# Another order of the passes, one streamed weight unit fewer and a ring of five places in a recurrent attention kernel

## The chip, the cores and the metric

The kernel runs on one core of one Trainium2 chip. A core has a matrix engine (TensorE, "PE" in the profile; "PEld" is its weight load), a vector engine (VectorE, DVE), a scalar engine (ScalarE, ACT), GpSimd (POOL) and SyncE (SP), which mostly issues transfers; 16 DMA engines move data between the chip's memory and the core's on-chip memory. Matmuls write to PSUM, eight banks of accumulator memory, from which VectorE and ScalarE copy. The metric is the device time of one execution in microseconds (us); lower is better.

## What is computed

The output is the sum of three things on a sequence of 2048 tokens of 1024 features: the input itself, a memory-augmented recurrent attention, and a dense layer with GELU. Cut to what matters:

```python
def _A_ref(x, mem0, Wq, Wk, Wv, Wo, seg_len):     # seg_len = 32, 64 segments, 32 heads of 128
    mem = mem0                                      # 8 rows
    for s in range(n_seg):
        h = jnp.concatenate([mem, xs], axis=1)      # 8 memory rows + 32 tokens
        q, k, v = (jnp.einsum('btd,dhe->bhte', h, W) for W in (Wq, Wk, Wv))
        scores = jnp.where(mask, jnp.einsum('bhqe,bhke->bhqk', q, k) * scale, -1e9)
        o = jnp.einsum('bhqk,bhke->bhqe', softmax(scores), v)
        o = jnp.einsum('bhte,hed->btd', o, Wo)
        mem = o[:, :M, :]                           # the next segment needs these 8 rows
        outs.append(o[:, M:, :])
xn = layernorm(x)
return x + _A_ref(xn, ...) + (gelu(xn @ w1 + b1) @ w2 + b2)
```

Every segment needs all of Wq, Wk, Wv and Wo (each 1024 x 4096 in bf16, 8 MB), and the memory rows of the segment before. So the 64 segments run one after the other, and 32 MB of weights pass TensorE in each.

## The kernel before, in words

**Stages.** First the layer norm and the dense layer over all tokens (L257 to L515), then the recurrence (L522 on), one segment after the other. The profile sees the recurrence begin some 360 us into the span, when its first weights are fetched.

**Rows.** A segment's "main" rows are 24 of its tokens and the 8 memory rows, 32 in all. Its last 8 tokens, the "left" rows, are done for four segments at once, in a batch of 32 rows: the left keys in a group's segment 0 (i4 = 0), the left queries of the first half of the heads in segment 1, of the second half in segment 2, the left values in segment 3, and the output rows of a batch in segment 1 (`left_o`). A pass with left rows has twice the matmuls.

**Weight units.** The weights are cut into 64 units of 128 x 2048 bf16 (512 KB): eight for each of Q, K and V and each half u of the heads, and 16 for Wo. `ORDER` (L53 to L68) is the order in which a segment uses them: K, Q, V of half 0, then K, Q, V of half 1, then O. Most of them stay on chip. The 18 marked S in `PLACED` (L69) are streamed anew in every segment into a ring of six places (`STREAM_BUFS`, L50): when TensorE is done with a streamed unit, `unit_done` (L575) calls `start_stream` (L207), which issues the transfer of the unit that uses the same place next, on SP's queue (L215). One streamed unit, `IN_PSUM` (L74), lies transposed back in two PSUM banks (`kept`) and is copied to its place by ScalarE and VectorE (L212, L213) in place of a transfer.

**A pass.** `half_pass` (L634) multiplies the rows by eight units, four matmuls of 32 columns of the array side by side for each (L616), into a PSUM bank taken from a list of four (`new_acc`, `let_go`). `at` holds what is issued to the engines behind unit number i of a pass. Rows of K and Q leave PSUM by a ScalarE copy (L664; left rows by VectorE, L670) into a home on chip, where VectorE turns them (L679). The homes are `d_oL` and `b_oL`, which later hold the attention output, and `natQ`.

**Attention of a half.** `scores(u)` (L714) are matmuls into the bank `mixed` (L722, L728), the exponential on ScalarE (L733) and the masks on VectorE (L738); q's left columns come by L702, and L707 (`keep_q`) puts some aside. `sums` (L741) sums over keys by matmuls (L747), inverts by a logarithm and an exponential on ScalarE (L751, L752) and multiplies (L753, L754). `values(u, r)` (L756) multiplies by V, a quarter of the heads at a time, into two fresh banks, whose main and left columns are copied out by two instructions each (L776, L777).

**The order around the change.** scores(0) is issued behind unit 5 of V0, sums behind unit 2 of K1, the values of half 0 behind units 4 and 6 of Q1; scores(1) behind unit 5 of V1, sums of half 1 behind unit 1 of O, its values behind units 4 and 6 of O. Between segments the product's memory rows are copied (L873, L875), transposed by matmuls (`put_mem`, L247) and written into the next segment's rows `hr` (L251); three and three "lead" products of the next left pass (`lead_products`) are issued around them. `hr` has one buffer; its tokens are loaded by a transfer from POOL's queue (L223) issued behind V1.

Of the kernel before, what the change touches and what calls it, by code (L numbers as in the profile page):

```python
# [68 lines left out]
PLACED = "S....S.." "..S...S." "..S...S." "..S....S" "..S..S.." ".S...S.." "S...S..S" "...S..SS"  # L69
# [9 lines left out]
def kernel(  # L79
# [51 lines left out]
    natQ = nc.alloc_sbuf_tensor_at("natQ", [P, 512], BF16, offset=SCRATCH + 2048)  # L131
# [29 lines left out]
    for half in range(2):  # L161
        m = mask_left[0:SEG, :, 8 * half:8 * half + 8]
# [44 lines left out]
    def start_stream():  # L207
        nonlocal started
        if started < len(streams):
            t = slab(STREAM_PLACES[started % STREAM_BUFS])  # L210
            if streams[started] == IN_PSUM and "kept" in nxt:
                nc.scalar.copy(out=t[:, 0:1024], in_=nxt["kept"][:, 0, :])  # L212
                nc.vector.tensor_copy(out=t[:, 1024:2048], in_=nxt["kept"][:, 1, :])  # L213
            else:
                nc.sync.dma_start(out=t[:, :], in_=copies[streams[started]])  # L215
# [19 lines left out]
    b_oL = sp.tile([P, 1152], BF16, name="b_oL")  # L235
    HOME = {"d": d_oL[:, 0:512], "b": b_oL[:, 0:640]}
    o_main = [t.rearrange("p (h t) -> p h t", h=16) for t in (d_oL[:, 0:512], b_oL[:, 128:640])]
    o_both = [t.rearrange("p (t h) -> p h t", h=16) for t in (d_oL[:, :], b_oL[:, 128:1152])]

    def put_mem(o_sb, hT, ps, nb=4):  # L240

        nc_ = KT // nb
        rows = ident[:, :].rearrange("p (j t) -> p j t", j=nb)[:, :, NX:SEG]
        psM = ps[:, 0:8 * KT].rearrange("p (c j t) -> p c j t", c=nc_, j=nb)
        for c in range(nc_):
            for q in range(4):
                nc.tensor.matmul(  # L247
                    psM[32 * q:32 * q + 32, c, :, :], lhsT=o_sb[:, c * P + 32 * q:c * P + 32 * q + 32], rhs=rows,
# [9 lines left out]
    with tc.tile_pool(name="ma", bufs=2) as ma, tc.tile_pool(name="mps", bufs=6, space=PSUM) as mps:  # L258
# [11 lines left out]
        o_sb = HOME["d"]  # L270
        nc.vector.memset(o_sb[:, 0:256], 0.0)
# [10 lines left out]
        for j in range(4):  # L282
            nc.sync.dma_start(out=o_sb[32 * j + NX:32 * j + 32, 0:256], in_=mem0[:, 256 * j:256 * j + 256])
# [67 lines left out]

        def with_left(seg):
# [3 lines left out]
        def turn_R(ttg, small=None):  # L356
# [3 lines left out]
            for i in range(4):  # L360
# [8 lines left out]
                if with_left(seg):  # L369
                    pairs = [(both[w][0:SEG, :, :], halves[w]) for w in range(2)]  # L370
                else:
                    pairs = [(hr_d[seg + 1, :, 256:512].rearrange("(j t) c -> t j c", j=4), rows)]
                for sl in (slot, slot ^ 2) if seg in (0, 1, NSEG - 2, NSEG - 1) else (slot,):
                    r0 = SEG + NL * sl
# [147 lines left out]
    with tc.tile_pool(name="late", bufs=1) as late, \  # L522
# [28 lines left out]
        def keep_unit(t):  # L551

            for n in range(4):
                for k in range(4):
                    nc.tensor.transpose(tr[:, k, :], t[:, 512 * n + P * k:512 * n + P * (k + 1)], ident[:, :])
                turned = HOME["b"][:, 0:512].rearrange("p (k t) -> p k t", k=4)
# [34 lines left out]
        for t in o_both:  # L591
            nc.vector.memset(t[:, :, 32:64], 0.0)
        for s in range(NSEG):
# [13 lines left out]
            og, slot = divmod(s + 2, GRP)  # L607
            st = {}
# [48 lines left out]
            def home(tag, pool=sp):  # L657
                if tag in HOME:
                    return HOME[tag][:, 0:512]
                return natQ[:, :] if tag == "n" else pool.tile([P, 512], BF16, name="natL", tag=tag)[:, :]  # L660

            def rows_out(ps, tag):
                nat = home(tag)
                nc.scalar.copy(out=nat[:, :], in_=ps[:, :])  # L664
                let_go(ps)
                return nat

            def left_out(psL, tag, pool=sp):
                nat = home(tag, pool)
                nc.vector.tensor_copy(out=nat[:, :], in_=psL[:, :])  # L670
                let_go(psL)
                return nat

            def left_values(u, ps):
                VL[u] = left_out(ps, f"VL{u}", late)

            def turn(out, nat):

                nc.vector.transpose(out=out, in_=nat.rearrange("p (h e) -> p h e", e=32))  # L679

            def turn_k(ps):
                st["kT"] = sp.tile([P, 16, 32], BF16, name="kT", tag="a")
                turn(st["kT"][:, :, :], rows_out(ps, "d"))

            def turn_kL(ps, u):
                kL[u] = sp.tile([P, 16, 32], BF16, name=f"kL{u}")
                turn(kL[u][:, :, :], left_out(ps, "d"))

            def turn_q(ps, tag):
                st["qT"] = HOME["b"].rearrange("p (h q) -> p h q", q=40)  # L690
                turn(st["qT"][:, :, 0:32], rows_out(ps, tag))

            def turn_qL(ps, u, tag):
                turn(qL[:, u, :, :], left_out(ps, tag))

            def q_left(u):
# [5 lines left out]
                nc.vector.tensor_copy(out=st["qT"][:, :, 32:40], in_=q)  # L702
# [11 lines left out]
            def scores(u):  # L714

                kT, qT = st["kT"], st["qT"]
                sA = mixed[:, 0:160].rearrange("p (c q) -> p c q", q=40)
                sB = mixed[:, 160:224].rearrange("p (c q) -> p c q", q=16)
                for c in range(4):
                    for j in range(4):  # L720
                        q = slice(32 * j, 32 * j + 32)
                        nc.tensor.matmul(  # L722
                            sA[q, c, :], lhsT=kT[:, 4 * c + j, :], rhs=qT[:, 4 * c + j, :],
                            start=(c == 0), stop=True, skip_group_check=True, tile_position=(0, 32 * j),
                        )
                    for j in range(4):
                        q = slice(32 * j, 32 * j + 32)
                        nc.tensor.matmul(  # L728
                            sB[q, c, :], lhsT=kL[u][:, 4 * c + j, :], rhs=qT[:, 4 * c + j, NX:40],
                            start=False, stop=True, skip_group_check=True, tile_position=(0, 32 * j),  # L730
                        )
                pr = sp.tile([P, 224], BF16, name="pr", tag="e")
# [3 lines left out]
                for p, m in ((prA[:, :, 0:NX], mask_order), (prB, mask_left[:, i4, :])):  # L736
                    n = m.shape[-1]
                    nc.vector.tensor_tensor(out=p, in0=p, in1=m[:, None, :].to_broadcast([P, 4, n]), op=ALU.min)  # L738
                st["prA"], st["prB"] = prA, prB

            def sums():  # L741
                prA, prB = st["prA"], st["prB"]
                dA = mixed[:, 0:160].rearrange("p (c q) -> p c q", q=40)
                for p, d, b in ((prA, dA, True), (prB, dA[:, :, NX:40], False)):
                    for j in range(4):
                        q = slice(32 * j, 32 * j + 32)
                        nc.tensor.matmul(  # L747
                            d[q, :, :], lhsT=bd[:, q], rhs=p, start=b, stop=not b, skip_group_check=True,
                            tile_position=(0, 32 * j),
                        )  # L750
# [3 lines left out]
                nc.vector.tensor_tensor(out=prB, in0=prB, in1=dA[:, :, NX:40], op=ALU.mult)  # L754

            def values(u, r):  # L756

                V, prA, prB = st["V"], st["prA"], st["prB"]
                av = [new_acc() for _ in range(2)]
                oV = [t[:, 0:160].rearrange("p (c q) -> p c q", q=40) for t in av]  # L760
                for c in range(4):
# [6 lines left out]
                    for b in range(2):  # L768
                        q = slice(64 * r + 32 * b, 64 * r + 32 * b + 32)
                        nc.tensor.matmul(  # L770
                            oV[b][:, c, NX:40], lhsT=VL[u][q, c * P:(c + 1) * P], rhs=prB[q, c, :],
                            start=False, stop=True, skip_group_check=True, tile_position=(64 * r + 32 * b, 0),
                        )
                for b, cp in enumerate((nc.scalar.copy, nc.vector.tensor_copy)):
                    hs, t0 = slice(8 * r + 4 * b, 8 * r + 4 * b + 4), SEG + NL * slot
                    cp(out=(o_both if left_o else o_main)[u][:, hs, 0:32], in_=oV[b][:, :, 0:32])  # L776
                    cp(out=o_both[u][:, hs, t0:t0 + NL], in_=oV[b][:, :, 32:40])  # L777
                    let_go(av[b])

            def o_product(unit, t, acc):  # L780
# [3 lines left out]
                lhs = o_both[i // 4] if left_o else o_main[i // 4]  # L784
# [14 lines left out]
            turn_k(psK)  # L799
# [3 lines left out]
            turn_q(psQ, "d")  # L803
            if left_q[0] and first:
                turn_qL(psQL, 0, "d")
            q_left(0)
            psV, psVL = half_pass("V", 0, left_v, {5: [lambda: scores(0)]})
            st["V"] = left_out(psV, "b")
            if first:
                left_values(0, psVL)  # L810


            at = {2: [sums]}
            if left_q[0] and not first:
                at[5] = [lambda: keep_q(0), lambda: turn_qL(psQL, 0, "d")]
            psK1, psK1L = half_pass("K", 1, left_k, at)
            turn_k(psK1)
            if left_k:
                if more and not first:
                    load_left_rows(g + 1, nc.gpsimd)  # L820
                turn_kL(psK1L, 1)
            at = {4: [lambda: values(0, 0)], 6: [lambda: values(0, 1)]}
            if left_v and not first:
                at[6].append(lambda: left_values(0, psVL))
            psQ1, psQ1L = half_pass("Q", 1, left_q[1], at)
            turn_q(psQ1, "n")
            if first:
                turn_qL(psQ1L, 1, "n")
            q_left(1)
            at = {5: [lambda: scores(1)]}  # L830
            if left_q[1] and not first:
                at[2] = [lambda: keep_q(1), lambda: turn_qL(psQ1L, 1, "n")]
# [16 lines left out]
            st["V"] = left_out(psV1, "a")  # L849
# [8 lines left out]
            at = {1: [sums], 4: [lambda: values(1, 0)], 6: [lambda: values(1, 1)]}  # L858
# [12 lines left out]
            if not final:  # L871
                o_sb = HOME["d"]
                nc.scalar.copy(out=o_sb[:, 0:256], in_=psX[:, 0:256])  # L873
                if left_o:
                    nc.vector.tensor_copy(out=o_sb[:, 256:512], in_=psX[:, 256:512])  # L875
# [8 lines left out]
                put_mem(o_sb, nxt["hT"], mixed[:, 256:512], 4 // nw)  # L884
# [81 lines left out]
```

## Time and profile before

| what | value |
|---|---|
| three runs | 2080.75, 2083.34, 2098.01 us; median 2083.34 |
| the profiled execution | 2073.2 us |
| its span, first to last instruction | 2071.5 us |
| mean granted clock of TensorE | 0.98 |
| PE busy | 1814.4 us (88%), 34291 matmuls |
| DVE, ACT, POOL busy | 976.9 (47%), 655.8 (32%), 270.9 us (13%) |
| moved by DMA | 661 MB, mean 319 GB/s |
| chain that ended last | PE 60%, DMA 19%, DVE 9%, ACT 7%, issue 4% |

The profile is of one execution, so durations in it are added up against its own time, not against the median. A row of instructions gives line, engine, operation, output <- input, count, then busy us and mean ns of one, then the idle time of the engine before them and what ended most of it. Since matmuls overlap in TensorE, a mean of 386 ns for a matmul is its passage, not its share of the time. A row of waits gives who waited for whom, in total us, times and the longest one. In the windows, the clock is that granted to TensorE as a share of full speed, and the DMA share is the mean busy share of the 16 DMA engines.

### The profile page before, as it was taken

How to read it: one execution, taken by the hardware profiler on the slowest of the kernel's cores; microseconds unless marked ns; L12 is line 12 of the kernel's file. 1: busy time of each engine (PE TensorE's matmuls, PEld its weight loads, DVE VectorE, ACT ScalarE, POOL GpSimd, SP SyncE). 2: the span in 40 equal slices, each digit the busy share in tenths (PEclk: the TensorE clock that was granted, in tenths of full speed). 3: DMA queues.
4: the chain of work that ended last, by engine and by line, in shares of the span. 5: the costliest groups of instructions: out<-in, count | busy, mean ns of one | idle time of the engine just before them, and what ended most of it. 6: DMA issues, size and time to landing. Idle time of an engine off the chain costs nothing.

```text
span 2071.5 us, 77587 instructions
## 1 busy us (share of the span) xinstructions
PE 1814.4 (88%) x34291; PEld 1034.7 (50%) x34291; DVE 976.9 (47%) x2553; ACT 655.8 (32%) x1540; POOL 270.9 (13%) x528
## 2 busy tenths in 40 slices
PE   6999999978888888888889888879888888888887
PEld 3444444445555555554555555545555555455554
DVE  6665657134444444444444444444444444444443
ACT  4342525113232323232323332223332323232332
POOL 0000000004411111111111111111111111111111
PEclk9999999999999999999999999999999999999999
DMA  9721212899999999999999999999999999999998
GB/s 328 246 56 38 59 39 60 311 343 369 386 369 367 377 360 370 363 388 341 370 363 382 381 369 355 350 366 366 364 370 339 356 352 379 350 367 355 373 361 330
DMA packets 228974, 661.17 MB, mean 319 GB/s; under 512 B 47851, under 2 KB 65211, under 8 KB 228636
## 3 DMA queue, kind: packets, MB, share of 16 engines
q1 hardware_dynamic: 207100, 636.04, 82.4%
q0 software_dynamic: 16000, 16.87, 2.5%
q8 instruction: 268, 4.39, 0.8%
q10 hardware_dynamic: 5536, 3.30, 0.5%
q14 instruction: 70, 0.57, 0.1%
HBM read 641.85 MB, written 31.52 MB: 325 GB/s over the span
## 4 chain that ended last, share of the span: by engine, by line
PE 60%; DMA 19%; DVE 9%; ACT 7%; issue 4%; ACTq 0%; POOL 0%; DVEq 0%; POOLq 0%; SPq 0%
PE acc L616 23%; PE acc L788 12%; PE ps L419 9%; DMA u<-Wc_O 8%; PE ps L467 7%; DMA u<-Wc_Q 4%; ACT d_oL L664 2%; DVE b_oL L679 2%; PE acc L764 2%; DMA res<-hr_d 2%; DMA outM_d<-res 2%; PE ps L500 2%; ACT d_oL L776 2%; DVE d_oL L670 1%; DVE kT L679 1%
## 5 line engine op out<-in xcount | busy, mean ns | idle before, releaser
L616 PE MATMUL acc<-u,hr 128*32 128x512 bf16 x11520 | 808.0, 386 | 41.4 <-DMA u<-Wc_Q 13.8
L616 PEld LDWEIGHTS <-hr 128*32 128x32 bf16 x12288 | 360.2, 97 | 317.8 <-issue 83.7
L616 PE MATMUL acc<-u,hrL 128*32 128x512 bf16 x2880 | 260.5, 388 | 5.0 <-issue 5.0
L664 ACT CAST d_oL<-acc 128x512 bf16<-128x512 f32 x192 | 112.4, 585 | 385.9 <-PE acc L616 316.6
L419 PE MATMUL ps<-u 128*128 128x512 bf16 x896 | 195.4, 381 | 2.6 <-ACT u L325 2.6
L679 DVE STREAM_TRANSPOSE kT<-d_oL 128x512 bf16<-128x512 bf16 x128 | 91.3, 713 | 198.5 <-ACT d_oL L664 198.5
L788 PEld LDWEIGHTS <-b_oL 128*32 128x32 bf16 (+1 forms) x3552 | 141.6, 119 | 60.2 <-issue 49.9
L788 PE MATMUL acc<-u,d_oL 128*32 128x256 bf16 (+1 forms) x2220 | 142.9, 299 | 19.5 <-issue 10.3
L788 PEld LDWEIGHTS <-d_oL 128*32 128x32 bf16 (+1 forms) x3552 | 118.7, 112 | 60.2 <-issue 25.0
L467 PE MATMUL ps<-u 128*128 128x512 bf16 x672 | 147.0, 379 | 0.0
L788 PE MATMUL acc<-W_O,b_oL 128*32 128x256 bf16 (+1 forms) x2220 | 124.1, 308 | 22.7 <-issue 22.7
L419 PEld LDWEIGHTS <-u 128*128 128x128 bf16 x896 | 87.9, 98 | 108.8 <-issue 4.3
L738 DVE TENSOR_TENSOR pr<-pr,beside 128x96 bf16<-128x96 bf16 (+1 forms) x256 | 49.0, 232 | 156.1 <-ACT pr L733 156.1
L733 ACT ACTIVATE pr<-mixed 128x224 bf16<-128x224 f32 x128 | 45.7, 357 | 236.7 <-PE mixed L728 174.8
L616 PEld LDWEIGHTS <-hrL 128*32 128x32 bf16 x3072 | 89.8, 97 | 51.9 <-issue 13.6
L213 DVE COPY u<-kept 128x1024 bf16<-128x1024 bf16 x63 | 43.6, 692 | 146.0 <-ACT u L212 143.5
L467 PEld LDWEIGHTS <-u 128*128 128x128 bf16 x672 | 65.3, 98 | 77.3 <-DVE g_u L435 0.4
L788 PE MATMUL acc<-u,b_oL 128*32 128x256 bf16 (+1 forms) x1332 | 88.2, 309 | 16.4 <-DMA u<-Wc_O 10.2
L223 POOL DMA_DIRECT2D hr<-hr_d x63 | 34.6, 549 | 516.8 <-PE acc L616 325.9
L928 POOL DMA_DIRECT2D out_dram<-res x124 | 63.2, 516 | 254.2 <-DVE res L890 253.3
L427 ACT ACTIVATE g_xb<-ps,b1col 128x512 bf16<-128x512 f32 x112 | 76.8, 686 | 60.4 <-PE ps L419 59.3
L212 ACT COPY u<-kept 128x1024 bf16<-128x1024 bf16 x63 | 63.8, 1012 | 91.3 <-PE acc L788 86.7
(123 smaller groups left out, 2377.5 us busy)
## 6 DMA issues: line engine op xcount, KB each, us to landing
u<-Wc_O SPq DMA_DIRECT2D x384, 512.0 KB
u<-Wc_K SPq DMA_DIRECT2D x256, 512.0 KB
u<-Wc_V SPq DMA_DIRECT2D x256, 512.0 KB
u<-Wc_Q SPq DMA_DIRECT2D x193, 512.0 KB
u<-in_B_w_dram SPq DMA_DIRECT2D x16, 448.0 KB
u<-in_B_w_dram SPq DMA_DIRECT2D x14, 512.0 KB
u<-in_A_Wq_dram SPq DMA_DIRECT2D x12, 512.0 KB
u<-in_A_Wv_dram SPq DMA_DIRECT2D x12, 512.0 KB
```

The source lines that it names most:

```text
L212: nc.scalar.copy(out=t[:, 0:1024], in_=nxt["kept"][:, 0, :])
L213: nc.vector.tensor_copy(out=t[:, 1024:2048], in_=nxt["kept"][:, 1, :])
L419: nc.tensor.matmul(ps[:, :].rearrange("p (s t) -> p s t", t=SEG), lhsT=w1_sb[fb // 14 * 8 + kt][:, (fb % 14) * P:(fb % 14 + 1) * P], rhs=x ...
L427: nc.scalar.activation(out=xb[:, :], in_=ps[:, :], func=ACT.Identity, bias=b1col[:, fb:fb + 1], scale=1.0)
L467: nc.tensor.matmul(ps[:, :], lhsT=gts[fc // 4][:, fc % 4, t * P:(t + 1) * P], rhs=w2_sb[fc // 2][:, fc % 2, cs], start=(fc == 0), stop=(fc ...
L616: nc.tensor.matmul(o, lhsT=lhs[:, i, :], rhs=m, start=(i == seq[0]), stop=(i == seq[-1]), tile_position=(0, 32 * j),)
L664: nc.scalar.copy(out=nat[:, :], in_=ps[:, :])
L679: nc.vector.transpose(out=out, in_=nat.rearrange("p (h e) -> p h e", e=32))
L733: nc.scalar.activation(out=pr[:, :], in_=mixed[:, 0:224], func=ACT.Exp, scale=INV_SQRT_DH)
L738: nc.vector.tensor_tensor(out=p, in0=p, in1=m[:, None, :].to_broadcast([P, 4, n]), op=ALU.min)
L788: nc.tensor.matmul(acc[r:r + n // 8, 0:n], lhsT=lhs[:, 4 * (i % 4) + 2 * u + k, :], rhs=t[:, 1024 * k + n * jq:1024 * k + n * jq + n], sta ...
L928: nc.gpsimd.dma_start(out=out_flat[rows, 256 * j:256 * j + 256], in_=res[32 * j:32 * j + NX, :])
```

## The change

It sets the order of a segment's passes to K0, Q0, K1, Q1, V0, V1, O; with it the points move at which scores, sums and values are issued. It streams 17 units in a ring of five places instead of 18 in one of six, with new places for them in the order; the place gained holds one more resident unit. The low end of the on-chip memory (`SCRATCH`, for the descriptors of POOL's transfers, and `SMALL`) is cut anew, `natQ` goes, and V of half 0 and the weights `pr` of half 1 get places of their own (`v_home`, `pr_last`). Rows of K and Q of both halves pass one home, `nat_home`, a part of `d_oL`; the turned queries lie in a part of `b_oL` (`q_home`), left ones ahead of main ones. The attention output of left and main rows lies side by side (`outs`), so that one copy takes both out of PSUM and O's weights are contiguous. The second values call of a half (and both in segment 3) takes half of the bank `mixed` in place of one fresh bank. V leaves PSUM by ScalarE instead of VectorE; both copies of the unit kept in PSUM go by VectorE; the residual of segment 2 is loaded by POOL instead of ScalarE.

The core of the diff:

```diff
-STREAMED = 18
+STREAMED = 17
-SCRATCH = 1024
-SMALL = 3072
+SCRATCH = 576
+SMALL = 3520
-STREAM_BUFS = 6
+STREAM_BUFS = 5
...
-    for u in range(2):
-        for w in ("K", "Q", "V"):
-            for i in range(KT):
-                order.append((w, i, u))
+    for w, u in (("K", 0), ("Q", 0), ("K", 1), ("Q", 1), ("V", 0), ("V", 1)):
+        for i in range(KT):
+            order.append((w, i, u))
...
-PLACED = "S....S.." "..S...S." "..S...S." "..S....S" "..S..S.." ".S...S.." "S...S..S" "...S..SS"
+PLACED = "S....S.." "..S....S" "....S..." "S....S.." ".S....S." "..S..S.." "S..S..S." "..S..S.S"
...
-                nc.scalar.copy(out=t[:, 0:1024], in_=nxt["kept"][:, 0, :])
-                nc.vector.tensor_copy(out=t[:, 1024:2048], in_=nxt["kept"][:, 1, :])
+                for b in range(2):
+                    nc.vector.tensor_copy(out=t[:, 1024 * b:1024 * b + 1024], in_=nxt["kept"][:, b, :])
...
-    b_oL = sp.tile([P, 1152], BF16, name="b_oL")
+    b_oL = sp.tile([P, 1024], BF16, name="b_oL")
+    outs = [t.rearrange("p (h t) -> p h t", h=16) for t in (d_oL, b_oL)]
+    nat_home, q_home = outs[0][:, :, 32:64], outs[1][:, :, 24:64]
...
+            def rows_out(ps, out, cp):
+
+                cp(out=out, in_=ps.rearrange("p (h e) -> p h e", e=32))
                 let_go(ps)
...
+            def turn_q(ps):
+                rows_out(ps, nat_home, nc.scalar.copy)
+                turn(q_home[:, :, NL:40])
+
+            def turn_qL(ps, u):
+                rows_out(ps, nat_home, nc.vector.tensor_copy)
+                turn(qL[:, u, :, :])
...
+            def ends(t):
+
+                return t.rearrange("p c (a b) -> p c a b", b=NL)[:, :, ::4, :]
...
-                av = [new_acc() for _ in range(2)]
+                low_bank = r == 1 or (left_v and not first)
+                av = [mixed[:, 256:512] if low_bank and b == 0 else new_acc() for b in range(2)]
...
-                    cp(out=(o_both if left_o else o_main)[u][:, hs, 0:32], in_=oV[b][:, :, 0:32])
-                    cp(out=o_both[u][:, hs, t0:t0 + NL], in_=oV[b][:, :, 32:40])
+                    cp(out=outs[u][:, hs, NL * slot:NL * slot + 40], in_=oV[b])
...
             psK, psKL = half_pass("K", 0, left_k, {})
-            turn_k(psK)
+            rows_out(psK, nat_home, nc.scalar.copy)
+            turn_k()
             if left_k:
                 turn_kL(psKL, 0)
             psQ, psQL = half_pass("Q", 0, left_q[0], {})
...
+            psK1, psK1L = half_pass("K", 1, left_k, {})
+            rows_out(psK1, nat_home, nc.scalar.copy)
...
+            at = {0: [lambda: scores(0), turn_k], 6: [lambda: sums(0)]}
+            if left_k:
+                at[1] = [lambda: turn_kL(psK1L, 1)]
+            psQ1, psQ1L = half_pass("Q", 1, left_q[1], at)
+            turn_q(psQ1)
...
+            psV, psVL = half_pass("V", 0, left_v, {})
+            st["V", 0] = values_out(psV, v_home, nc.scalar.copy)
...
+            at = {0: [lambda: scores(1)], 2: [lambda: values(0, 0)], 4: [lambda: values(0, 1)], 6: [lambda: sums(1)]}
             if left_v and not first:
-                at[6].append(lambda: left_values(0, psVL))
...
+                at[4].append(lambda: left_values(0, psVL))
...
-            if i4 in (0, 3) and not final and not first:
-                at[4] = [lambda: load_res("rs", nc.gpsimd)]
+            if i4 != 1 and not final and not first:
+                at[5] = [lambda: load_res("rs", nc.gpsimd)]
             psV1, psV1L = half_pass("V", 1, left_v, at)
...
-            at = {1: [sums], 4: [lambda: values(1, 0)], 6: [lambda: values(1, 1)]}
+            at = {4: [lambda: values(1, 0)], 6: [lambda: values(1, 1)]}
```

The rest of the diff fits masks, `put_mem`, the residual rows and the output rows to the new layout.

More of the change, by code (lines that the diff above doesn't have):

```diff
@@ L802 @@
             psQ, psQL = half_pass("Q", 0, left_q[0], {})
-            turn_q(psQ, "d")
-            if left_q[0] and first:
-                turn_qL(psQL, 0, "d")
+            turn_q(psQ)
+            if first:
+                turn_qL(psQL, 0)
             q_left(0)
-            psV, psVL = half_pass("V", 0, left_v, {5: [lambda: scores(0)]})
-            st["V"] = left_out(psV, "b")
+            if left_q[0] and not first:
+                keep_q(0)
+                turn_qL(psQL, 0)
+            psK1, psK1L = half_pass("K", 1, left_k, {})
@@ new lines @@
+            rows_out(psK1, nat_home, nc.scalar.copy)
+            if left_k and more and not first:
+                load_left_rows(g + 1, nc.gpsimd)
+            at = {0: [lambda: scores(0), turn_k], 6: [lambda: sums(0)]}
[3 more added lines that the diff above has]
+            turn_q(psQ1)
+            if first:
+                turn_qL(psQ1L, 1)
+            q_left(1)
+            if left_q[1] and not first:
+                keep_q(1)
+                turn_qL(psQ1L, 1)
```

167 lines of the change are left out of this document (77 added, 90 removed).

## The prediction

> **What bounds the kernel now.** First the page of the profile, to see which part of the span counts.
>
> ```profile
> span 2071.5 us, 77587 instructions
> DMA  9721212899999999999999999999999999999998
> ```
>
> From the eighth slice on the DMA engines are busy in nine tenths or more: that is the recurrence, four fifths of the span. The change touches nothing that costs time before it. The line of the copy that closes a segment (L873) gives its period.
>
> ```profile
> L873 ACT CAST d_oL<-acc x63: 372/372/379, 467.8 to 2041.3; 128x256 bf16<-128x256 f32 x63
> ```
>
> 63 closings from 467.8 to 2041.3 us are 62 periods of **25.4 us**. The windows table (its columns: PE, PEld, DVE, ACT, POOL busy, granted TensorE clock, DMA share, GB/s) shows that the stage is even, and, in a narrow window, a thing that the mean hides.
>
> ```profile
> 400.00:800.00 400.00, 341.20 (x7372) 201.38 (x7374) 172.34 (x446) 112.14 (x285) 79.06 (x146) 0.98 0.97 361
> 800.00:1200.00 400.00, 346.83 (x8056) 205.90 (x8044) 182.52 (x485) 123.21 (x320) 56.62 (x107) 0.98 0.98 369
> 1200.00:1600.00 400.00, 342.61 (x7940) 207.16 (x7936) 178.95 (x476) 119.43 (x311) 56.85 (x107) 0.97 0.97 361
> 1600.00:2000.00 400.00, 344.12 (x7904) 209.44 (x7900) 177.90 (x476) 119.97 (x312) 56.30 (x106) 0.97 0.97 360
> ...
> 1066.50:1070.90 4.40, 3.06 (x105) 2.30 (x100) 1.94 (x7) 1.26 (x5) 0.54 (x1) 1.00 1.02 390
> 1070.90:1074.40 3.50, 3.50 (x75) 2.81 (x76) 0.68 (x3) 1.48 (x3) 0.00 (x0) 0.51 0.96 357
> ```
>
> Two resources are near their end. The DMA share is 0.97 to 0.98, so a period holds 0.972 x 25.4 = **24.7 us of transfer work**. PE is busy 1374.8 of 1600 us: 21.8 us of a period, idle 3.6. What ends that idle time is in the list of waits of PE between 400 and 2000 us (total, times, longest):
>
> ```profile
> PE acc L788 <- issue: 42.3, 34, 2.6
> PE acc L764 <- ACT d_oL L777: 36.6, 30, 1.5
> PE mixed L722 <- DVE b_oL L702: 35.7, 67, 1.5
> PE acc L788 <- DMA u<-Wc_O: 17.2, 33, 1.5
> PE acc L764 <- DVE pr L753: 14.9, 34, 0.5
> PE acc L616 <- DMA u<-Wc_Q: 12.4, 30, 1.3
> PE mixed L747 <- DVE pr L738: 11.9, 14, 1.9
> PE acc L616 <- issue: 7.9, 13, 2.2
> PE acc L616 <- DMA u<-Wc_V: 6.5, 10, 1.0
> PE acc L616 <- ACT d_oL L777: 6.2, 29, 0.2
> PE acc L616 <- DMA u<-Wc_K: 5.8, 7, 1.6
> ```
>
> 1600 us are 63 periods. Streamed weights: 17.2 + 12.4 + 6.5 + 5.8 = 41.9, **0.66 us** a period. Other engines: 36.6 + 35.7 + 14.9 + 11.9 + 6.2 = 105.3, **1.67 us**. "Issue", which waits for nothing that shows: about 0.9 us. So without any weight wait PE would need 25.4 - 0.66 = 24.7 us, as much as the transfers need. Both are the bound, and the 0.7 us above either is what two equal servers lose to each other over a ring.
>
> **The change, part by part.**
>
> *One streamed unit less.* 17 of 18 streamed units come by DMA now (one is kept in PSUM), 16 of 17 afterwards. A unit is 512 KB; 361 GB/s at share 0.97 is 372 GB/s for fully busy engines, so a unit is 0.524 MB / 372 = 1.41 us of work. Transfer work falls from 24.7 to **23.3 us**. At the present share a period could not be under 23.3 / 0.972 = 23.9 us. The extra resident unit is loaded in the first segment in place of being streamed there: no bytes more or less.
>
> *The waits of PE that go.* Scores wait for the turned Q (L722 on L702): they ran six units behind the Q pass, now nine. Values wait for a bank (L764, L616 on L777): the second values call now takes half of "mixed" as a bank, and one 40-wide copy replaces the two of L776 and L777. Sums and values of the second half (L747, L764 on L738, L753): sums(1) moves before the O product, and the weights tile "pr" no longer shares a place with a result still being written out. I take all 1.67 us as removed; the bounds are 0.8 and 1.67.
>
> *The waits that come.* All rows and queries of K and Q now pass one home, nat_home, one after the other. The durations:
>
> ```profile
> L664 ACT CAST d_oL<-acc 128x512 bf16<-128x512 f32 x192 | 112.4, 585 | 385.9 <-PE acc L616 316.6 <-DVE kL L679 35.6 <-DVE qL L679 31.5
> L679 DVE STREAM_TRANSPOSE kT<-d_oL 128x512 bf16<-128x512 bf16 x128 | 91.3, 713 | 198.5 <-ACT d_oL L664 198.5
> L670 DVE CAST d_oL<-acc 128x512 bf16<-128x512 f32 x48 | 33.0, 688 | 3.4
> L702 DVE COPY b_oL<-qL 128x128 bf16<-128x128 bf16 x83 | 12.8, 154 | 0.1
> L707 DVE CAST beside<-qL 128x256 f32<-128x256 bf16 x15 | 6.3, 421 | 0.0
> L733 ACT ACTIVATE pr<-mixed 128x224 bf16<-128x224 f32 x128 | 45.7, 357 | 236.7 <-PE mixed L728 174.8 <-DMA outM_d<-res 27.5 <-PE acc L616 20.9
> L738 DVE TENSOR_TENSOR pr<-pr,beside 128x96 bf16<-128x96 bf16 x128 | 32.2, 251 | 156.1 <-ACT pr L733 156.1
> L738 DVE TENSOR_TENSOR pr<-pr,beside 128x64 bf16<-128x64 bf16 x128 | 27.4, 214 | 0.0
> L751 ACT ACTIVATE mixed<-mixed 128x160 f32<-128x160 f32 x128 | 36.9, 288 | 150.6 <-PE mixed L747 150.6
> ...
> 1001.57 4.14 PE acc L616 x76
> ```
>
> 76 matmuls in 4.14 us are 0.054 each, so a unit of four is 0.22 and a pass of 32 is 1.74; scores take 0.2.
> Segment 1 of a group (left queries in Q0): after Q0 the home is taken for 0.59 + 0.71 + 0.15 + 0.42 + 0.69 + 0.71 = 3.3 us. K1 ends after 1.74, so its ACT copy starts 1.5 us late; queued behind it on ACT is the exponential of scores(0), and behind that DVE's masks: 3.3 + 0.59 + 0.36 + 0.25 + 0.21 and hand-overs = 4.8. PE reaches sums(0) at 1.74 + 0.2 + 7 x 0.22 = 3.5: **1.3 us** of wait.
> Segment 0 (left keys): after K1 DVE does masks, turn_k, the left copy and its turn, until about 3.5 us; Q1's ACT copy waits for that home (its pass ended at 2.05), then 0.59 + 0.71 + 0.15 make the queries ready at 5.0. PE comes to scores(1) at 2.05 + 1.74 + 0.22 = 4.0: **1.0 us**.
> The other two have about 0.0 to 0.3 us to spare there, since Q1's copy queues on ACT behind sums(0)'s two functions (0.29 each): 0.1. Together (1.3 + 1.0) / 4 + 0.1 = **0.7 us** a period; bounds 0.3 and 1.1.
>
> *The next segment's rows.* hr has one buffer; POOL asks for it when V1 ends.
>
> ```profile
> hr<-hr_d POOLq DMA_DIRECT2D x63, 64.0 KB, 5.5
> ...
> 1041.10:1047.70 6.60, 4.93 (x176) 4.18 (x168) 2.82 (x10) 2.13 (x7) 0.54 (x1) 1.00 1.05 391
> ```
>
> It lands 5.5 us after its issue, some 6 us after V1. The O stage of this row took 6.6 us and hid it. Without sums and bank waits O needs 16 x 0.22 = 3.5 us, two values calls and the lead products (1.3 us), about 5.3. If weights are ready, up to 0.9 us shows; but six of O's units are streamed and pace it. I take 0.3 (bounds 0, 0.9).
>
> *Edits that I cost at nothing.* The kept unit's two halves are copied so now:
>
> ```profile
> L213 DVE COPY u<-kept 128x1024 bf16<-128x1024 bf16 x63 | 43.6, 692 | 146.0 <-ACT u L212 143.5
> ...
> L212 ACT COPY u<-kept 128x1024 bf16<-128x1024 bf16 x63 | 63.8, 1012 | 91.3 <-PE acc L788 86.7
> ```
>
> Both go by DVE afterwards, 2 x 0.69 in place of 1.01 and 0.69 one behind the other. The pair starts two units before O ends and is done 1.0 us after it, where PE still has six lead products (1.3 us); with that cover gone, in the last group, it is 0.3 us for four segments. V's copy on ACT (0.59) is not needed before PE is three units on. The weights of the O product lie side by side now: its matmuls run at 0.107 to 0.114 us already, so 0 to 0.1 a period. Split operands of 2 x 8 have counts and sizes as before. One more load on POOL in segment 2 is queued ahead of hr's but issued two units before V1 ends, and an issue is 0.54 (POOL's only work in the row from 1041.10).
>
> *The half clock.* In the row from 1070.90 the granted clock is 0.51 right behind a stretch in which PE was busy 3.06 of 4.40 us. Mean clocks of 0.97 and 0.98 say that 5% of the stage ran so: 1.27 us of a period at half speed, 0.6 lost. Shorter gaps should spare half: **-0.3 us** (bounds 0, -0.6).
> The Trainium skill ("TensorE: Matmul & The Clock Gate", "The HAM clock gate") has the half clock follow a window of some 3.4 us of idle PE. The trace disagrees, since no wait in the list above is longer than 2.6 us; by that rule this term would be 0 and the sum 0.3 x 62 = 19 us higher.
>
> *Sum.* PE without weight waits: 24.7 - 1.67 + 0.7 + 0.3 - 0.3 = **23.7 us**; transfers 23.3. The loss between them was 0.7 with equal loads and six places. Loads 0.4 apart lower it, five places raise it by up to 6/5: I keep **0.7** (bounds 0.5 and 1.0). Period 24.4, gain 1.0 x 62 = **62 us**. The profiled execution took 2073.2 us around its span, 10 under the median of the runs, 2083.34; so 2011 for such an execution, and **2021 us** for the median. The low bounds together end at the transfers' 23.9. The high ones together would go past today's 25.4; halfway there lies B's 25.2 below, and I let the range end with it.
>
> **The rivals.**
> *A, transfers alone decide*: PE's waits vanish as hoped and the period is 23.9: 1.5 x 62 = 93, 1990 us. For it: the share is already 0.97. Against: PE then must stay under 23.2.
> *B, no relief of PE*: one home gives back what the banks gained, PE stays at 24.7, and with 0.5 between them the period is 25.2: 12 us, 2071. For it: the two long chains above. Against: they strike two segments in four.
> *C, the ring of five is too shallow*: slower. The chain of waits shows what a late unit took, from place freed to weights landed:
>
> ```profile
> 1007.96 7.74 DMA u<-Wc_V
> ```
>
> A turn of the ring is 6 x 25.4 / 18 = 8.5 us now; at a period P it will be 5P / 17. Use and issue take 8.5 - 7.7 = 0.8. If landing still takes 7.1 us, P = (7.1 + 0.8) x 17 / 5 = 26.9: 93 us more, 2176; if 6.9, 26.2, 2133. It decides from 25.4, a landing of 6.7 us. Against: four transfers in flight instead of five should shorten 7.7 to some 6.2 (four fifths). The Trainium skill ("DMA: Bandwidth & Descriptors", "Anatomy of one DMA") gives about 2.0 us plus bytes over 436 GB/s, by which a lone unit would land in an estimated 3.2 us and the ring would not bind; no run here shows a lone one.
>
> **How the numbers follow.** My forecast 0.52, A 0.20, B 0.17, C 0.11. A measurement of this kernel tells about 1% from no change (its three runs span 0.8%). Faster by over 1% (under 2062): forecast, A and a little of B, 0.75; within 1%: most of B, 0.15; slower: 0.10. The range runs from just under A, 1985, to just over B, 2072; C lies outside.
>
> **What would show it.** Right: period near 24.4, streamed units by DMA 16 a segment, waits for L777 and L702 gone, new waits of sums on the masks in segment 1 and of scores on queries in segment 0, "issue" as before. Wrong: a DMA share under 0.94 with weight waits over 1.2 us a period (C); other-engine waits still over 1.5 (B); a period of 23.9 or less (A).

## The result, and the profile after

The changed kernel takes 2031.33 us (median of four runs, 2029.69 to 2037.55) beside 2082.99 us before: a ratio of 0.9743, 95% interval 0.9693 to 0.9793. (It is the ratio of the means; that of the medians is 0.975.) The forecast was 2021, in a range from 1985 to 2072. One execution of an experiment below, the old order with seven places, was a slow one of 3375.1 us and is left out of its median and its ratio.

The page and the closing copy's line of the changed kernel (its lines have other numbers: L893 for L873, L628 for L616, L808 for L788):

```profile
span 2028.5 us, 77105 instructions
...
DMA  9821212789899999999999999999999999999998
...
L893 ACT CAST d_oL<-acc x63: 372/372/374, 468.1 to 1998.3; 128x256 bf16<-128x256 f32 x63
```

The recurrence begins where it did, and 62 periods take 1530.2 us: **24.68 us** a period against 25.38. The windows, with the columns of before:

```profile
400.00:800.00 400.00, 342.70 (x7374) 184.48 (x7376) 146.69 (x376) 97.39 (x243) 80.79 (x149) 0.97 0.93 343
800.00:1200.00 400.00, 350.91 (x8236) 196.86 (x8232) 158.44 (x414) 109.41 (x276) 61.12 (x115) 0.98 0.96 355
1200.00:1600.00 400.00, 348.95 (x8228) 193.01 (x8221) 159.41 (x419) 109.54 (x279) 62.62 (x118) 0.98 0.97 355
1600.00:2000.00 400.00, 343.10 (x8232) 190.72 (x8235) 155.87 (x410) 109.41 (x278) 59.65 (x112) 1.00 0.98 360
```

The transfers have become slower: 343 to 360 GB/s, where they were 360 to 369, and that with fewer bytes to move (628 MB for 661). PE's waits between 400 and 2000 us:

```profile
PE acc L808 <- DMA u<-Wc_O: 83.1, 141, 2.1
PE acc L628 <- DMA u<-Wc_V: 25.8, 33, 1.6
PE acc L808 <- issue: 22.9, 25, 2.8
PE acc L628 <- DMA u<-Wc_Q: 18.8, 28, 3.0
PE mixed L733 <- DVE b_oL L709: 14.2, 15, 1.0
PE mixed L758 <- DVE pr L750: 10.3, 16, 1.9
PE acc L628 <- DVE hr L250: 8.5, 5, 3.7
...
PE acc L628 <- DMA u<-Wc_K: 1.1, 2, 0.5
```

The waits for banks are gone. Two new ones stand where the prediction put them, as a rule once in each group of four: scores for queries in segment 0 (15 times, 0.9 us each) and sums for masks in segment 1 (16 times, 0.6; two of them in segment 2). But the waits for weights tripled, from 41.9 us to 83.1 + 25.8 + 18.8 + 1.1 = 128.8, that is 2.0 us a period. Of the prediction's signs of being wrong, half of rival C's has come: weight waits over 1.2 us, but a DMA share under 0.94 in the first window alone.

### The profile page after: what moved, and what is told of

Same layout as the page of the kernel before. It is cut to its first block, busy times and chain, and to the rows that moved or that the text cites. A ratio compares the mean times of both kernels' runs of the same rounds, so it can differ in the third digit from the quotient of the medians.

```text
span 2028.5 us, 77105 instructions
## 1 busy us (share of the span) xinstructions
PE 1789.3 (88%) x34291; PEld 951.5 (47%) x34291; DVE 863.2 (43%) x2232; ACT 590.6 (29%) x1349; POOL 279.9 (14%) x544
## 3 DMA queue, kind: packets, MB, share of 16 engines
q8 instruction: 268, 4.39, 0.9%
## 4 chain that ended last, share of the span: by engine, by line
PE 53%; DMA 39%; issue 3%; DVE 3%; ACT 1%; POOL 1%; DVEq 0%; POOLq 0%; ACTq 0%; SPq 0%
DMA u<-Wc_O 23%; PE acc L628 23%; PE ps L430 10%; PE acc L808 8%; PE ps L478 7%; DMA u<-Wc_Q 7%; DMA u<-Wc_V 5%; DMA u<-Wc_K 2%; PE ps L511 2%; PE mixed L783 1%; DMA res<-hr_d 1%; PE pT L511 1%; DVE u L213 0%; PE pT L324 0%; ACT d_oL L671 0%
## 5 line engine op out<-in xcount | busy, mean ns | idle before, releaser
L628 PE MATMUL acc<-u,hr 128*32 128x512 bf16 x11520 | 799.7, 383 | 62.5 <-DMA u<-Wc_V 26.5
L628 PEld LDWEIGHTS <-hr 128*32 128x32 bf16 x12288 | 344.3, 97 | 364.4 <-issue 96.3
L671 ACT CAST d_oL<-acc 128x512 bf16<-128x512 f32 x256 | 150.3, 587 | 439.7 <-PE acc L628 350.8
L628 PE MATMUL acc<-u,hrL 128*32 128x512 bf16 x2880 | 257.1, 388 | 3.1 <-issue 3.0
L808 PEld LDWEIGHTS <-b_oL 128*32 128x32 bf16 (+1 forms) x3552 | 113.7, 102 | 110.8 <-issue 78.6
L808 PE MATMUL acc<-u,d_oL 128*32 128x256 bf16 (+1 forms) x2220 | 122.3, 295 | 42.3 <-DMA u<-Wc_O 38.3
L808 PEld LDWEIGHTS <-d_oL 128*32 128x32 bf16 (+1 forms) x3552 | 98.4, 99 | 103.4 <-issue 51.9
L808 PE MATMUL acc<-W_O,b_oL 128*32 128x256 bf16 (+1 forms) x2220 | 130.7, 300 | 11.6 <-issue 11.6
L213 DVE COPY u<-kept 128x1024 bf16<-128x1024 bf16 x126 | 81.2, 686 | 138.2 <-PE acc L808 111.2
L808 PE MATMUL acc<-u,b_oL 128*32 128x256 bf16 (+1 forms) x1332 | 92.4, 303 | 47.4 <-DMA u<-Wc_O 45.5
L684 DVE STREAM_TRANSPOSE b_oL<-d_oL 128x512 bf16<-128x512 bf16 x128 | 91.1, 712 | 73.1 <-ACT d_oL L671 70.5
L796 DVE CAST b_oL<-acc 128x160 bf16<-128x160 f32 x128 | 41.5, 325 | 174.4 <-PE acc L789 174.4
L628 PEld LDWEIGHTS <-hrL 128*32 128x32 bf16 x3072 | 85.4, 97 | 53.7 <-issue 17.9
L223 POOL DMA_DIRECT2D hr<-hr_d x63 | 34.5, 548 | 515.0 <-PE acc L628 451.6
L808 PE MATMUL acc<-W_O,d_oL 128*32 128x256 bf16 (+1 forms) x1332 | 92.2, 298 | 7.1 <-issue 7.1
```

What stands on the lines that cost most here:

```text
L213: nc.vector.tensor_copy(out=t[:, 1024 * b:1024 * b + 1024], in_=nxt["kept"][:, b, :])
L223: eng.dma_start(out=hr[:, :], in_=hr_d[s, :, 0:256])
L628: nc.tensor.matmul(o, lhsT=lhs[:, i, :], rhs=m, start=(i == seq[0]), stop=(i == seq[-1]), tile_position=(0, 32 * j),)
L671: cp(out=out, in_=ps.rearrange("p (h e) -> p h e", e=32))
L684: nc.vector.transpose(out=out, in_=nat_home)
L796: cp(out=outs[u][:, hs, NL * slot:NL * slot + 40], in_=oV[b])
```

## The experiments

Theory 1, the prediction's: PE is relieved by order and banks, and one streamed unit less lowers the bound of the transfers. Theory 2: the order alone brings the gain, and the ring's lost place costs what the streamed unit saves. Theory 3: the swap of a place for a unit brings it. Each ratio below is to the kernel before on the same chip; "new" is the order, homes and banks of the changed kernel with all its smaller edits; these were not tried one by one.

**The four corners.** The new order with six places, and the old one with five:

```diff
-STREAMED = 17
-STREAM_BUFS = 5
+STREAMED = 18
+STREAM_BUFS = 6
+PLACED: the positions of before
```

> The new order, homes and banks alone: 18 streamed units in six places, on the positions of before. Theory 1 (PE is relieved to some 22.7 us a period, the transfers are the bound): 24.7 us of transfer work a period must show, so 25.0 to 25.2, some 2050 to 2065 us. Theory 2 (the order alone brought the gain, the swap of a place for a streamed unit nothing): 2025 to 2040 us. Theory 3 (the swap brought all of it): 2075 to 2085 us.

Measured: 2022.47 us, ratio 0.9698 (0.9652 to 0.9744). One of its windows, with the share and rate that six places reach in the new order:

```profile
800.00:1200.00 400.00, 348.55 (x8316) 201.60 (x8316) 160.50 (x418) 109.40 (x278) 61.82 (x116) 0.99 0.99 379
```

```diff
-STREAMED = 18
-STREAM_BUFS = 6
+STREAMED = 17
+STREAM_BUFS = 5
+PLACED: the positions of after
```

> The swap alone, in the old order: 17 streamed units in five places, on the positions of after. Theory 1: PE without weight waits still needs 24.7 us and five places lose more than six did, so 25.4 to 25.9 a period, 2080 to 2115 us: nothing gained or slower. Theory 3 (one unit less is worth its 1.4 us whatever PE does): 2000 to 2040 us.

Measured: 2096.15 us, ratio 1.0034 (1.0007 to 1.0061). This excludes theory 3, and the run before it excludes theory 1 (2050 to 2065) as well; theory 2, which had 2025 to 2040 there, is left. The swap costs some 10 us in the old order (1 to 13 by the interval), and in the new one its two kernels' intervals overlap, the medians 9 us apart the same way. The new order with its homes and banks is the gain. The swap means place, unit and positions together; the positions by themselves were tried only further below, spread evenly.

**The depth of the ring alone.** A sixth and an eighth place, with 17 streamed units; the place comes from resident units that are read from another's tile:

```diff
-STREAM_BUFS = 5
+STREAM_BUFS = 6          # and 8
-        late_units = deque(RESIDENT[len(RES_PLACES):])
+        late_units = deque(RESIDENT[len(RES_PLACES):-1])   # and -3
+        for unit in RESIDENT[-1:]:
+            res_tiles[unit] = res_tiles[RESIDENT[0]]
```

> The changed kernel with a sixth place for the ring and 17 streamed units all the same; the place is had by letting the last resident unit (of Wo) be read from another unit's tile, so that unit is not loaded and its product is another one. The depth of the ring alone. If the two us of weight waits a period come from the shallow ring: 0.3 to 0.5 us a period less, 2000 to 2012 us. If the transfers' own rate sets them: within 5 us of 2031.

Measured: 1981.68 us, ratio 0.9498 (0.9452 to 0.9545): 50 us below the changed kernel, 0.7 us a period, more than either alternative had.

> The changed kernel with eight places and 17 streamed units; three resident units of Wo are read from another unit's tile and not loaded. The depth of the ring once more. A sixth place was worth 50 us. If depth is what holds the transfers back and PE alone needs 22.7 us a period: another 30 to 60 us, 1920 to 1950 us, weight waits of PE nearly gone. If six places are enough and the rest is rate: 1970 to 1982 us.

Measured: 1978.11 us, ratio 0.9529 (0.9471 to 0.9586): nothing beyond the sixth place, though the expected end of weight waits came (0.9 us for streamed units in 1200). What came in their place, in its list of waits between 400 and 1600 us:

```profile
PE acc L810 <- issue: 59.4, 33, 2.9
PE acc L630 <- issue: 19.5, 24, 1.7
PE mixed L760 <- DVE pr L752: 10.2, 16, 1.0
...
PE acc L810 <- DMA u<-Wc_O: 0.9, 2, 0.6
```

**PE alone, and the transfers alone.**

```diff
         if IS_STREAMED[unit]:
-            return stream_tiles.popleft()[:, :]
+            return res_tiles[RESIDENT[0]]
...
-        if started < len(streams):
+        if started < 0:
```

> The changed kernel without any streamed weight: the 17 units are read from a resident unit's tile, so their products are other ones and no transfer of theirs is issued. PE alone with its waits for other engines. Prediction's sum: 23.7 us a period, 1970 us. From the trace of the changed kernel (24.68 less 1.99 of weight waits): 22.7, some 1905 us; less if issue waits come from the transfers' load on the chip: 22.0, 1865 us.

Measured: 1747.6 us, ratio 0.8412 (0.8364 to 0.846), below every expectation. Its closing copies, one window, and all of its waits of PE over 2 us between 400 and 1600:

```profile
L893 ACT CAST d_oL<-acc x63: 372/372/373, 455.2 to 1719.8; 128x256 bf16<-128x256 f32 x63
...
800.00:1200.00 400.00, 391.00 (x9944) 228.57 (x9944) 164.58 (x459) 130.26 (x329) 73.98 (x139) 1.00 0.06 17
...
PE mixed L733 <- DVE b_oL L709: 13.6, 15, 1.0
PE mixed L758 <- DVE pr L750: 9.9, 14, 0.7
PE kept L571 <- DVE v_home L568: 2.1, 4, 0.5
```

PE alone needs **20.4 us** a period, at full clock, busy 98% of the time. "Issue" is not in the list: those waits come with the streamed weights. (The copies of the unit kept in PSUM, two of 0.69 us a period on VectorE, are left out here too.)

```diff
-                    product(w, i, t, hT, ps, range(KT))
-                    if left and i not in ahead:
+                    if IS_STREAMED[w, i, u] or i in (0, KT - 1):
+                        product(w, i, t, hT, ps, range(KT))
+                    if left and i not in ahead and (IS_STREAMED[w, i, u] or i in (order[0], order[-1])):
```

> The changed kernel with most of PE's products of resident units left out (of each pass only the first and last unit and the streamed ones are multiplied), all transfers as before: the transfers alone over five places. If their work is fixed at 23.3 us a period as the prediction had it: 23.3 to 23.9, 1945 to 1980 us. If the rate follows the number in flight, which is largest when PE always waits: 21.8 to 22.8, 1855 to 1915 us.

Measured: 2008.56 us, two runs, ratio 0.9668 (0.9611 to 0.9725): above both expectations.

```profile
L894 ACT CAST d_oL<-acc x63: 372/372/373, 471.4 to 1980.3; 128x256 bf16<-128x256 f32 x63
...
800.00:1200.00 400.00, 287.87 (x6356) 149.00 (x6349) 161.75 (x428) 111.40 (x283) 65.05 (x122) 0.85 0.98 361
```

With a quarter of its matmuls in a period gone (387 left of 508, from the windows of 800 to 1200 us) PE is busy 72% of the time and waits 5.8 us a period for weights (283.6 us between 400 and 1600), and the period is still **24.3 us**. A turn of the ring is then 5 x 24.34 / 17 = 7.16 us, of which 6.4 pass on average from a unit's issue to its landing. Leaving out that part of PE's work saves 0.35 us: 16 transfers over five places hold the changed kernel's period. (PE's clock is at 0.85 here, so this is an upper bound on what the transfers need.)

**One step the other way.** Seven places and 19 streamed units.

```diff
-STREAMED = 17
-STREAM_BUFS = 5
+STREAMED = 19
+STREAM_BUFS = 7
+PLACED = "S...S..." "S...S..S" "..S...S." ".S..S..." "S..S..S." "..S..S.." "S...S..S" "...S..S."
```

> A whole kernel with the new order and seven places for 19 streamed units, one step further the other way than the change went (six and 18 took 2022 us, five and 17 2031). If a place is still worth more than a unit costs: 2005 to 2018 us. If 18 units by transfer are then too many for the rate (18 x 1.38 us at 380 GB/s is 24.8 and the small ones): 2035 to 2070 us.

Measured: 2071.81 us, ratio 0.9947 (0.992 to 0.9974). The last place is not worth its unit. It moves bytes faster than any other:

```profile
800.00:1200.00 400.00, 343.61 (x8057) 190.21 (x8052) 153.51 (x405) 105.41 (x268) 59.30 (x111) 0.99 1.01 388
```

**Is the old order bound by its transfers?** It gets a seventh place.

```diff
-STREAM_BUFS = 6
+STREAM_BUFS = 7          # and one resident unit from another's tile, as above
```

> The kernel before with a seventh place for its 18 streamed units (the last resident unit of Wo is read from another unit's tile and not loaded). If its transfers were the bound at their full rate, as the prediction read their share of 0.97: within 10 us of 2083. If their rate follows the places that come free in time, as in the new order: 30 to 50 us less, 2035 to 2055 us.

Measured: 2088.83 us, ratio 1.0036 (1.0008 to 1.0064): no gain. Its waits between 400 and 1600 us:

```profile
PE acc L790 <- issue: 30.7, 24, 2.4
PE mixed L724 <- DVE b_oL L704: 29.0, 52, 1.5
PE acc L766 <- ACT d_oL L779: 27.2, 22, 1.5
PE mixed L749 <- DVE pr L740: 25.2, 27, 3.9
PE acc L766 <- DVE pr L755: 12.9, 28, 0.7
...
PE acc L790 <- DMA u<-Wc_O: 8.7, 12, 1.5
```

Weight waits fall from 0.7 to 0.2 us a period, and the waits for other engines grow by as much. So depth alone did not hold the old order; its waits point to PE's chain with the other engines. The step is not quite the one that brought 50 us in the new order: from six places to seven with 17 units by DMA, there from five to six with 16.

**Where the streamed units stand.** Evenly over the 64 units, in the ring of five and in that of six; for the latter also without the double small transfers, with the positions of before and evenly.

```diff
+PLACED = "S...S..." "S..SS..." "S...S..." "S...S..." "S...S..." "S...S..." "S...S..." "S...S..."     # five places
+PLACED = "S...S..." "S.SS...S" "...S...S" "..S...S." "..S...S." ".S...S.." ".S...S.." "S...S..."     # six places
-            for _ in range(2 if len(small) > 8 else 1):
+            for _ in range(1):
```

> The changed kernel (five places, 17 streamed units) with the streamed units spread evenly, four in O in place of six; nothing else. 83 of its 129 us of weight waits stand in O. If the places cost them: 2005 to 2020 us. If the ring of five does wherever they stand: within 6 us of 2031, the waits moved to other passes.

Measured: 2129.15 us, ratio 1.0225 (1.0178 to 1.0271). Far off, and the wrong way.

> The same with the 18 streamed units spread evenly over the 64 (four of them among the 16 of O in place of six). PE's weight waits stand in O and V0 or V1, where the streamed units lie closest. If their places are what costs: weight waits halved, 1995 to 2008 us. If the transfers' rate and the number of places set the period: within 6 us of the same kernel with the positions of before.

Measured: 2124.12 us, ratio 1.02 (1.0156 to 1.0243), against 2020.03 us with the positions of before (below). Windows of the ring of five show what became longer. Of each pair the first is K to V, the second O. First the changed kernel, two segments, then the even one:

```profile
1018.20:1034.80 16.60, 15.91 (x376) 8.23 (x372) 6.20 (x18) 5.20 (x13) 1.81 (x3) 1.00 0.96 362
1034.80:1041.60 6.80, 5.29 (x172) 3.98 (x168) 2.56 (x7) 1.58 (x6) 0.54 (x1) 1.00 1.01 377
1041.60:1058.80 17.20, 15.70 (x376) 7.96 (x372) 8.40 (x21) 5.07 (x12) 3.15 (x6) 1.00 0.94 332
1058.80:1066.80 8.00, 5.25 (x168) 3.97 (x164) 2.30 (x6) 1.67 (x5) 0.53 (x1) 1.00 1.03 396
```

```profile
1054.20:1075.20 21.00, 16.65 (x376) 7.87 (x372) 6.14 (x17) 5.20 (x13) 1.82 (x3) 1.00 0.96 345
1075.20:1080.80 5.60, 4.74 (x170) 3.87 (x164) 2.82 (x7) 1.57 (x5) 0.54 (x1) 1.00 0.88 300
1080.80:1099.60 18.80, 16.69 (x376) 8.32 (x372) 8.04 (x21) 5.18 (x12) 3.16 (x6) 1.00 0.90 323
1099.60:1108.20 8.60, 6.38 (x168) 4.75 (x167) 2.39 (x6) 1.67 (x5) 0.54 (x1) 0.80 0.80 315
```

With four streamed units in O the DMA share falls to 0.88 and 0.80 there, and K to V pays 1.6 to 4.4 us for 1.2 saved or less. Over 50 segments of each trace it is the same: K to V 19.7 us for 16.9, O 6.4 for 7.6, the rate in O 325 GB/s for 377. Six in O keep the transfers at 1.01 to 1.03. That few places come free in O, and that PE's waits there are the price of the six and not the loss, is the reading that fits; which single move of a unit costs the time was not tried.

**POOL's queue in the early segments.** Segments 3 and 4 of the changed kernel took 29.1 and 31.0 us. POOL's timeline in segment 3 has the next rows (L223) behind a string of small transfers; they are asked for 5.8 us after V1's last matmul, where later segments ask within 0.5:

```profile
539.97 1.12 POOL L391 DMA_DIRECT2D hr_d<-R_n  x2
541.11 0.55 POOL L391 DMA_DIRECT2D hrL_d<-R_n  x1
541.93 0.58 POOL L862 DMA_DIRECT2D res<-hr_d  x1 [0.27 <-issue]
544.82 0.56 POOL L223 DMA_DIRECT2D hr<-hr_d  x1 [2.31 <-PE acc L808]
```

> The changed kernel with one small transfer behind each streamed unit on POOL's queue, never two. In the changed kernel's trace segments 3 and 4 take 29.1 and 31.1 us, where the rows of the next segment are asked for late behind a dozen such transfers. If that queue is the cause: both at about 24.5, 8 to 11 us less, 2020 to 2023 us. If they are late for another reason: 2031 us, the two segments as long as before.

Measured: 2024.78 us, ratio 0.9698 (0.9639 to 0.9756), an interval that overlaps the changed kernel's. One of the two segments came down to 23.5 us, the other only to 27.5. So the small transfers are at most a part of the cause: the 2.31 us for which POOL idles right before L223 in the lines above are not explained.

> A whole kernel: the new order with six places and 18 streamed units, positions of before, and one small transfer behind each streamed unit on POOL's queue. Six and 18 took 2022 us, and the one small transfer was worth some 6 us in the ring of five. If both add up: 2012 to 2018 us, faster than the kernel before and the changed one. If the early segments are late for the depth of the ring and not for POOL's queue: 2022 us.

Measured: 2020.03 us, ratio 0.9697 (0.9664 to 0.9731). Not told apart from the 2022.47 us without it. It is the fastest whole kernel here: its five runs (2015.04 to 2021.79) lie under the changed kernel's four (2029.69 to 2037.55), on another chip, while the two ratio intervals overlap.

## Why the prediction was right in its time and wrong in a step

The sums of the lists of waits of PE between 400 and 1600 us, by kind, and PE's busy time there, over the periods in 1200 us, show the trade (us a period):

| kernel | places, units by DMA | period | PE busy | weights | issue | other engines |
|---|---|---|---|---|---|---|
| before | 6, 17 | 25.4 | 21.8 | 0.7 | 0.9 | 1.8 |
| old order, 7 places | 7, 17 | 25.5 | 21.7 | 0.2 | 1.1 | 2.3 |
| old order, 5 places | 5, 16 | 25.8 | 21.9 | 1.2 | 0.6 | 2.0 |
| new order | 6, 17 | 24.7 | 21.3 | 1.5 | 1.2 | 0.6 |
| **changed kernel** | 5, 16 | 24.7 | 21.4 | 1.9 | 0.6 | 0.6 |
| six places | 6, 16 | 24.0 | 21.2 | 0.4 | 1.6 | 0.7 |
| eight places | 8, 16 | 23.9 | 21.1 | 0.1 | 2.0 | 0.6 |
| no stream | 0 | 20.4 | 19.9 | 0 | 0 | 0.5 |

Each row is one profiled execution; that of "new order" was the slowest of its four, 10 us over their median, so its period is 0.2 too long.

- *PE's waits that go and come*: right in kind, too small in size. 1.67 us were to go and 1.0 to come, so a net 0.7; waits for other engines fell from 1.8 to 0.6, by 1.2. The two long chains sit in segments 0 and 1 as forecast (0.9 us each time for the forecast 1.0; 0.6 for 1.3). The late rows cost 8.5 us in all instead of 0.3 a period, most of it in segments 3 and 4, where POOL asks for them late.
- *One streamed unit less*: the step that failed. Transfer work was to fall by 1.41 us and "five places raise it by up to 6/5: I keep 0.7", so the shallow ring was to cost nothing. The loss, PE's weight waits, measured 1.9; the place is worth 50 us by the depth experiment, and the swap as a whole gained nothing in either order. The sum of transfer work was not the fault: 0.965 x 24.7 is 23.8 us, beside the 23.3 forecast. The fault was to read the share of 0.97 as a bound. By that rule six places with 17 transfers could not be under 24.7 / 0.972 = 25.4 us; the new order does it in 24.7, at a share of 0.99 and 378 to 379 GB/s in the windows from 800 us on to 1600.
- *How many are in flight*: from SyncE's issue to the last signal of its landing a streamed unit took 6.5 us on average before, 6.2 in the changed kernel and 7.8 with seven places and 18 units by DMA (400 to 1600 us). Times units over the period that is 4.4, 4.0 and 5.5 units in flight, beside a mean of 364, 351 and 381 GB/s in the three windows. So the rate rises with the number in flight, but not with it alone: the even ring of six had 4.6 at 352.
- *The two bounds*: PE "without weight waits" was to need 23.7; the changed kernel's 24.7 less 1.9 are 22.8. The forecast took 1.0 off PE, and 1.9 came off: 1.2 of waits for other engines, about 0.35 of "issue", 0.35 of busy time. But the old order with seven places shows that taking a wait off need not take its time off: 0.5 us of weight waits became 0.5 of others. PE alone needs 20.4. Of the 4.3 us between, 1.9 are weight waits, 0.6 "issue", 0.2 other engines, and 1.5 are PE busy for longer (21.4 for 19.9) with the same matmuls. Some 0.5 of these are the half clock, granted for 1.05 us of a period in the changed kernel and for none without streamed weights; the rest is open.
- *The half clock*: granted 0.97, 0.98, 0.98 and 1.00 against 0.98, 0.98, 0.97 and 0.97. That spares about 0.2 us, for 0.3, nearly all of it in the last window; in the experiments that stream weights and leave out no product the time at half clock goes from 0.4 to 1.6 us a period, so 0.2 is within their scatter. By the Trainium skill's rule ("TensorE: Matmul & The Clock Gate", "The HAM clock gate") nothing should have been spared, as PE idled for no whole window before either (its longest wait was 2.6 us).
- So two errors cancel, and the time came out right in part by luck: 0.9 more came off PE than forecast, and the ring lost 1.2 more. By medians the new order alone brought 64 us, 1.0 a period, and the swap took 0.1 to 0.2 of it back. Rival C had the right mechanism, in the depth, and the wrong size: it drew a landing of 6.9 to 7.1 us from one late unit, and the mean of 6.2 gives (6.2 + 0.8) x 17 / 5 = 23.8 us. The formula that C's paragraph takes from the Trainium skill ("DMA: Bandwidth & Descriptors", "Anatomy of one DMA") is fitted there for transfers issued by GpSimd; these are issued by SyncE.

What "issue" is, the traces' records of packets tell. The page's "instruction" queue q8 carries 268 packets, 4.39 MB, and PE has 34291 matmuls and as many weight loads: 256 of PE's instructions a packet. Between 400 and 1600 us every "issue" wait of PE in every trace (35 in the changed kernel, 76 with eight places) stands a multiple of 256 of these instructions behind the one before, to within two. Each ends 1.1 to 1.7 us after a packet of this queue has ended; of PE's other waits about a tenth do. So PE waits there for its own instructions. A packet takes 1.0 us with streamed weights or without, but it starts late: 3.0 us (median) behind the first instruction of a block of 256 with eight places, 2.7 in the changed kernel, 0.4 without streamed weights. That explains why eight places bring nothing over six: weight waits go, and waits for instructions (2.0 us) take their place. That the packets queue behind the weights on the DMA engines would fit, but was not tried.

Not settled: whether the smaller descriptor region slows POOL, which part of the new order brings how much of the 64 us, and why the transfers are slower in K to V (346 GB/s over 50 segments of the changed kernel) than in O (377).

## What to carry to other kernels

A busy share near one need not be a bound: here shares of 0.96 to 0.99 stood beside 355 to 379 GB/s, and with eight places the share was 0.98 while PE hardly waited for weights. Before counting a transfer saved as time saved, ask how many are in flight and how soon a place comes free, and price the place given up against the unit taken out. Waits removed on one side of a ring can return on the other, and here also as waits for PE's own instructions; test the pair as two single changes. And a wait at the place where most units are streamed may be what keeps the transfers running; moving the units away can cost more than the wait.

## What was not expected of the hardware

The changed kernel moved 343 to 360 GB/s over five places, and 372 to 390 over seven with 19 streamed units. The Trainium skill ("DMA: Bandwidth & Descriptors", "Where 436 GB/s comes from") has about 358 GB/s, one core's share of its memory, bind such transfers, and names a measurement of 425 as well; the 388 of one core over 400 us are above the share, and the measurement decides. PE's instructions come by DMA too, and where weights are streamed they can be late: up to 2.0 us of a period of 23.9. Without streamed weights TensorE ran at its full clock, 98% busy, with no wait of the kind "issue" in 1200 us.
